# Seven half-size products for the second layer of a first mixture, with its weights narrowed in place

## The chip, the cores and the metric

The kernel runs on one core of one Trainium2 chip. The metric is the device time of one execution in microseconds (us); the number given for a kernel is the median of several executions.

## What is computed

Attention with a cluster mask, then a dense two-layer mixture (the "first mixture"), then a mixture of eight experts. Cut to what matters here:

```python
x = attention(q, k, v, centroids)            # (1536, 512)
h = x @ w_in                                  # w_in  (512, 2048)
g = h * (1.0 / (1.0 + np.exp(-h)))
x = g @ w_out                                 # w_out (2048, 512)
for e in range(8):                            # second mixture
    out += P[:, e:e+1] * (np.maximum(x @ w1[e], 0.0) @ w2[e])
```

All products are made in fp32 precision by splitting each factor into a part that TensorE's fp32r format holds and a rest: hi·hi + hi·lo + lo·hi, three matmuls for each product.

## The kernel before, in words

**Stages.** After the attention (L157 to L634) comes the first mixture, cut into NS1 = 4 blocks of 512 of the 2048 hidden features. A block is a loop over `u` (L1296): steps 0 to 6 are the first layer, steps 7 to 18 the second. Then follows the second mixture (L1353 on).

**First layer of a block.** The product of 512x512 weights with 512x1536 tokens is made by Strassen's scheme in Winograd's form: seven products of half size (256x256 by 256x768) in place of eight. `aproduct` (L679) issues one, 24 matmuls (L674); `AORD` (L131) is their order. `mfactor` (L145) makes a product's weight factor: `hi` by a ScalarE copy, `lo` by a VectorE subtraction. `sums1`, `sum4` and `sum3` (L135 to L143) make the weight sums on VectorE. `aevac` (L688) takes a product's three PSUM banks into the hidden blocks `hblk`, by ScalarE copies or VectorE additions. Products share PSUM sets of three banks: 1, 6, 7 and 4 one, 5 and 3 another, 2 a third.

**Second layer of a block.** Twelve output tiles (`ytile`, L724) of 512 columns by 128 features over all of the block's 512 hidden features, 12 or 16 matmuls each (L728), the ordinary product. `gsilu`, `ghi` and `glo` (L702 to L716) apply SiLU and split the hidden blocks. `total` (L743) adds a tile into the accumulator `acc1`: by ScalarE copies in block 0, by VectorE additions after that.

**Weights.** Each quarter of a weight block (128x512 values, `w_raw`, L81) is loaded by SyncE into one of three buffers and "narrowed" (`w_steps`, L89): the 64-bit numbers that the input holds become fp32 by bit operations. Steps `w0` (ScalarE, absolute value), `w1` (GpSimd, max and min), `w2` and `w3` (VectorE, shift and merge), `wb` and `wp0` (GpSimd, the low bits and their addition); for the second layer's weights then `wh` and `wp2`, the split.

**Order.** The instruction order on TensorE, VectorE, ScalarE and GpSimd is written out by hand: `put(s, u, f, ...)` (L755) hangs a step on slot `u` of block `s`, and the loop at L1295 issues slot after slot; each engine works through its own queue in that order and waits on semaphores. In the loop before, slots issue `mfactor`, `aevac` and `total` by rules (L1312 to L1321), then the hung steps, then the slot's product or tile.

Of the kernel before, what the change touches and what calls it, by code (L numbers as in the profile page):

```python
# [18 lines left out]
P = 128  # L19
# [20 lines left out]
def attention_moe_kernel(ctx, tc, kq, vp, cent, w_in, w_out, w_gate, w1, w2, out):  # L40
# [31 lines left out]
    raws, utp = {}, [wip]  # L72
# [16 lines left out]
    def w_steps(n, k, a=None):  # L89
# [16 lines left out]
        if not early:
            ts = nc.gpsimd.tensor_scalar

        def tail():
            if early:  # L110
                nc.scalar.activation(low, low, AF.Copy, scale=2.0**-29)
            else:
                ts(out=low, in0=low, scalar1=2.0**-29, scalar2=1.0, op0=ALU.mult, op1=ALU.mult)

        return dict(
            wb=tail,
# [5 lines left out]
            wp1=lambda: None,  # L122
            wh=lambda hi, lo: nc.scalar.copy(hi, a),
            wp2=lambda hi, lo: nc.vector.tensor_tensor(out=lo, in0=a, in1=r(hi), op=ALU.subtract),
# [6 lines left out]
    AORD = (1, 5, 6, 3, 7, 2, 4)  # L131
    AWHERE = {1: a11, 5: a21, 6: wsum, 3: a21, 7: a11, 2: a12, 4: a22}
# [6 lines left out]
    def sum4():  # L139
        nc.vector.tensor_tensor(out=a21, in0=a12, in1=wsum, op=ALU.subtract)  # L140
# [503 lines left out]
    utp.append(pool(rctx, "ut2", bufs=1, side="right"))  # L644
# [4 lines left out]
    wo_h, wo_l = (wop.tile([P, 4, 512], F32R, name=f"wo{c}") for c in "hl")  # L649
# [28 lines left out]

    def aproduct(s, i):  # L679
        p = AORD[i]  # L680
        if p in (1, 5, 2):
            asets[s, p] = [mps.tile([P, 512], F32, name=f"l{s}_{p}_{u}", tag="s") for u in range(3)]
        ps = asets[s, {6: 1, 7: 1, 4: 1, 3: 5}.get(p, p)]
        multiply(ps, groups1(i, wfac.pop((s, i)), yf[p]), p in (1, 5, 2))
# [32 lines left out]

    CHUNKS = (0, 2, 1)
# [5 lines left out]
    def ytile(s, t):  # L724
# [5 lines left out]
        if c < 2:  # L730
            for k in range(4):
                go(ps, wo_h, k, gh[:, c, k, :512], k == 0)
                go(ps, wo_l, k, gh[:, c, k, :512])
                go(ps, wo_h, k, gl[k // 2, c][:, k % 2, :512], False, k == 3)
# [470 lines left out]
    def narrow(n, k, keys):  # L1205
        if (n, k) not in quarters:
            quarters[n, k] = steps.pop(k + 4, None) if n == 1 else None
            quarters[n, k] = quarters[n, k] or w_steps(n, k, None if n % 2 else win[:, :, k * P : (k + 1) * P])
        for key in keys.split():
            quarters[n, k][key](*((wo_h[:, k : k + 1], wo_l[:, k : k + 1]) if key in ("wh", "wp2") else ()))  # L1210
            m = 4 * n + k + 3
            if key == ("wp1", "wp2")[n % 2] and 6 < m < 8 * NS1:
                w_raw(m // 4, m % 4)

    for s in range(NS1):
        n = 2 * s + 1
        if s == 0:
            put(s, 0, mfactor, 0, 1)
            put(s, 0, narrow, n, 0, "wh")
            put(s, 0, narrow, n, 1, "wh")  # L1220
            put(s, 0, narrow, n, 0, "wp2")
            put(s, 0, sum4)
            put(s, 0, narrow, n, 1, "wp2")
            put(s, 0, narrow, n, 2, "wb w0 w1")
            put(s, 1, narrow, n, 2, "w2 w3 wp0")
            put(s, 1, sum3)
            put(s, 1, split, 7, xb)
            put(s, 2, narrow, n, 2, "wh wp1 wp2")
            put(s, 2, narrow, n, 3, "wb w0 w1")
            put(s, 3, narrow, n, 3, "w2 w3 wp0")  # L1230
            put(s, 3, split, 4, xd)
            put(s, 4, narrow, n, 3, "wh wp1 wp2")
        else:
            put(s, 0, narrow, n, 0, "wh wp1")
            put(s, 0, sum4)
            put(s, 0, narrow, n, 1, "w2 w3 wp0")
            put(s, 0, narrow, n, 0, "wp2")
            put(s, 1, sum3)
            put(s, 1, narrow, n, 1, "wh wp1 wp2")
            put(s, 1, narrow, n, 2, "wb w0 w1")  # L1240
            put(s, 2, narrow, n, 2, "w2 w3 wp0")
            put(s, 2, narrow, n, 3, "wb w0 w1")
            put(s, 3, narrow, n, 2, "wh wp1 wp2")
            put(s, 3, narrow, n, 3, "w2 w3 wp0")
            put(s, 4, narrow, n, 3, "wh wp1 wp2")
        put(s, 4, gsilu, 3)
        put(s, 4, ghi, 3)
        put(s, 5, glo, s, 3)
        put(s, 5, gsilu, 7)
        put(s, 5, ghi, 7)  # L1250
        put(s, 6, glo, s, 7)
        put(s, 6, gsilu, 2)
        put(s, 6, ghi, 2)
        put(s, 7, glo, s, 2)
        put(s, 8, ghi, 4)
        put(s, 8, glo, s, 4)
        if s < NS1 - 1:
            n += 1
            for k in range(4):
                u = 8 + 2 * k  # L1260
                put(s, u, narrow, n, k, "wb w0 w1")
                put(s, u + 1, narrow, n, k, "w2 w3 wp0")
                put(s, u + 2, narrow, n, k, "wp1")
            n += 1
            put(s, 14, narrow, n, 0, "wb w0")
            put(s, 15, narrow, n, 0, "w1")
            put(s, 15, mfactor, s + 1, 0)
            put(s, 16, sums1)
            put(s, 17, mfactor, s + 1, 1)
            put(s, 17, narrow, n, 0, "w2 w3 wp0")  # L1270
            put(s, 17, narrow, n, 1, "wb w0")
            put(s, 18, narrow, n, 1, "w1")
# [21 lines left out]
    with tc.manual_schedule(engines={ENG.PE, ENG.DVE, ENG.Activation, ENG.Pool}):  # L1294
        for s in range(NS1):  # L1295
            for u in range(19):  # L1296
                if (s, u) == (0, 7):
                    acc1 = accp.tile([P, KC, NTOK], F32, name="acc1", tag="acc")
                if (s, u) == (NS1 - 1, 7):
# [12 lines left out]
                if 1 <= u <= 4:  # L1312
                    mfactor(s, u + 1)
                if 1 <= u <= 7:
                    aevac(s, u - 1)
                    if u == 5:
                        mfactor(s, u + 1)
                elif u > 7:
                    total(s, u - 8)
                elif s:  # L1320
                    total(s - 1, 11)  # L1321
# [287 lines left out]
```

## Time and profile before

| | us |
|---|---|
| median of 3 runs | 1433.44 (1433.26 to 1433.53) |
| the profiled execution | 1433.5 |
| its span, first to last instruction | 1431.7 |
| TensorE busy in the span | 1417.9 (99%) |

The profile is one execution. Each engine is a row of instructions with start and length; lengths of neighbours on one engine overlap, so what an instruction costs its queue is the distance from its start to the next start where the next one didn't wait. "Releaser" is the engine and line whose end let a waiting instruction start.

### The profile page before, as it was taken

Reading aid. Unit: us, or ns where it says so; the run is one execution under the profiler, and the core shown is the slowest. Engines: PE = TensorE matmul, PEld = TensorE weight load, DVE = VectorE, ACT = ScalarE, POOL = GpSimd, SP = SyncE. Lnnn points to the kernel's source line nnn. Section 1 sums busy time; section 2 is a strip of 40 time slices with the busy share of each in tenths; the row PEclk is TensorE's granted clock in tenths of the full one; section 3 lists DMA queues with packets and bytes.
Section 4 is the critical chain, followed back from the end, with each engine's and each line's share of the span. In section 5 each row is a group of like instructions: output and inputs, shape, how many; then the busy total and the mean of one; then the engine's idle time right before and its main releaser. Section 6 shows DMA issues by size and latency. Waiting matters only on the chain.

```text
span 1431.7 us, 25259 instructions
## 1 busy us (share of the span) xinstructions
PE 1417.9 (99%) x9685; PEld 1286.9 (90%) x9685; DVE 1141.1 (80%) x1887; ACT 973.1 (68%) x1876; POOL 441.4 (31%) x417
## 2 busy tenths in 40 slices
PE   8999999999999999999999999999999999999998
PEld 5777778888888899999999999999999999999998
DVE  7778888566756999997878878778788787887878
ACT  7777777653625476757768587686776867867764
POOL 6677754355361001302232222120211211202112
PEclk9999999999999999999999999999999999999999
DMA  7665621121121037758698897786956958669577
GB/s 209 184 182 146 195 66 45 48 86 60 59 95 38 2 102 142 121 115 184 107 194 134 157 177 132 139 140 116 172 97 119 162 96 169 113 120 163 92 149 133
DMA packets 136313, 177.49 MB, mean 124 GB/s; under 512 B 6272, under 2 KB 108672, under 8 KB 136192
## 3 DMA queue, kind: packets, MB, share of 16 engines
q0 software_dynamic: 83856, 87.56, 40.5%
q1 hardware_dynamic: 51648, 87.85, 19.9%
q8 instruction: 76, 1.25, 0.4%
q10 hardware_dynamic: 688, 0.46, 0.1%
q14 instruction: 45, 0.37, 0.1%
HBM read 65.36 MB, written 88.87 MB: 108 GB/s over the span
## 4 chain that ended last, share of the span: by engine, by line
PE 93%; DVE 3%; ACT 1%; issue 1%; POOL 1%; DMA 0%; DVEq 0%; POOLq 0%; ACTq 0%
PE b L674 27%; PE a L674 23%; PE y L728 9%; PE l L674 8%; PE b L1060 4%; PE q L1040 4%; PE t L349 4%; PE av L372 4%; PE r L1040 4%; PE s L305 2%; PE s L307 2%; DVE m L314 1%; POOL p L340 1%; DVE acc L1141 1%; DVE al L772 0%
## 5 line engine op out<-in xcount | busy, mean ns | idle before, releaser
L674 PE MATMUL b<-wfh,ah 128*128 128x256 f32 x1164 | 330.7, 284 | 0.1
L674 PE MATMUL b<-wfh,al 128*128 128x256 f32 x1164 | 329.2, 283 | 0.0
L674 PE MATMUL b<-wfl,ah 128*128 128x256 f32 x1164 | 329.2, 283 | 0.0
L1167 POOL DMA_DIRECT2D out_dram<-acc x87 | 126.5, 1779 | 535.2 <-ACT acc L1158 509.9
L1158 ACT ACTIVATE acc<-b,Pg 128x256 f32<-128x256 f32 x564 | 222.2, 538 | 6.2 <-PE b L1060 5.2
L674 PEld LDWEIGHTS b<-wfh,ah 128*128 128x128 f32 x1164 | 222.9, 192 | 0.5 <-ACT acc L1158 0.3
L674 PEld LDWEIGHTS b<-wfl,ah 128*128 128x128 f32 x1164 | 223.1, 192 | 0.0
L674 PEld LDWEIGHTS b<-wfh,al 128*128 128x128 f32 x1164 | 223.1, 192 | 0.0
L674 PE MATMUL a<-xfl,wfh 128*128 128x512 f32 (+1 forms) x640 | 215.8, 337 | 0.0
L674 PE MATMUL a<-xfh,wfl 128*128 128x512 f32 (+1 forms) x640 | 215.5, 337 | 0.0
L674 PE MATMUL a<-xfh,wfh 128*128 128x512 f32 (+1 forms) x640 | 215.4, 337 | 0.0
L1093 ACT CAST ah<-h 128x768 fp32r<-128x768 f32 x160 | 134.7, 854 | 111.1 <-DVE h L1189 53.3
L1080 ACT COPY h<-a 128x512 f32<-128x512 f32 x192 | 113.6, 618 | 102.4 <-PE a L674 96.7
L772 DVE TENSOR_TENSOR al<-h,ah 128x768 fp32r<-128x768 f32 x160 | 151.4, 954 | 28.8 <-ACT ah L1093 23.7
L674 PEld LDWEIGHTS a<-xfh,wfl 128*128 128x128 f32 x640 | 121.0, 189 | 13.0
L674 PEld LDWEIGHTS a<-xfh,wfh 128*128 128x128 f32 x640 | 121.1, 189 | 11.5 <-issue 0.6
L674 PEld LDWEIGHTS a<-xfl,wfh 128*128 128x128 f32 x640 | 121.0, 189 | 10.4
L323 ACT ACTIVATE p<-s,m 128x768 f32<-128x768 f32 x96 | 86.5, 903 | 35.2 <-DVE m L314 30.8
L340 POOL TENSOR_SCALAR p<-p,rec 128x768 f32<-128x768 f32 x95 | 85.8, 915 | 51.5 <-DVE rec L328 40.9
L314 DVE TENSOR_REDUCE m<-s 128x1 f32<-128x768 f32 x96 | 90.0, 951 | 13.9 <-PE s L307 13.5
L769 DVE TENSOR_TENSOR h<-q,h 128x384 f32<-128x384 f32 x112 | 61.0, 555 | 35.4 <-PE q L1040 33.1
L772 DVE TENSOR_TENSOR wfl<-w0r,wfh 128x512 fp32r<-128x512 f32 x96 | 64.6, 688 | 28.7 <-ACT wfh L885 28.7
(256 smaller groups left out, 3370.0 us busy)
## 6 DMA issues: line engine op xcount, KB each, us to landing
out_dram<-acc POOLq DMA_DIRECT2D x91, 768.0 KB, 9.1
w0r<-in_w_dram SPq DMA_DIRECT2D x16, 1024.0 KB, 5.6
w1r<-in_w_dram SPq DMA_DIRECT2D x16, 1024.0 KB, 8.6
qk<-qk SPq DMA_DIRECT2D x45, 192.0 KB, 3.5
wr<-in_w_in_dram SPq DMA_DIRECT2D x16, 512.0 KB, 3.8
wr<-in_w_out_dram SPq DMA_DIRECT2D x16, 512.0 KB, 3.5
first_out<-acc POOLq DMA_DIRECT2D x10, 768.0 KB, 8.6
raw<-in_kq_dram SPq DMA_DIRECT2D x16, 384.0 KB, 4.4
```

Of the source, the lines that this page charges most:

```text
L314: nc.vector.tensor_reduce(out=m, in_=tiles[i]["s"][:, :S], axis=AX.X, op=ALU.max, negate=True)
L323: nc.scalar.activation(t["p"], t.pop("s")[:, :S], AF.Exp, bias=t.pop("m"), accum_out=chunks[c]["sum"][:, j, 0:1])
L340: e.tensor_scalar(out=p, in0=p, scalar1=chunks[c]["rec"][:, j : j + 1], scalar2=1.0, op0=ALU.mult, op1=ALU.mult)
L674: nc.tensor.matmul(ps[u][:, cols], lhsT=lf(i, k), rhs=rt(j, k), start=fresh and u not in opened, stop=k == 1 and q == 2, skip_group_check= ...
L728: nc.tensor.matmul(out, lhsT=w[:, k, d * P : (d + 1) * P], rhs=g, start=first, stop=last, skip_group_check=True)
L769: e.tensor_tensor(out=out, in0=in0, in1=in1, op=op)
L772: e.tensor_tensor(out=lo, in0=x, in1=r(hi), op=ALU.subtract)
L1040: nc.tensor.matmul(ps, lhsT=quad_lhs(s, q, a, four), rhs=(x4 if four else xq)[b][:, XQ[q]], start=j == 0 and q in (1, 2, 5), stop=j == 2, ...
L1080: act.copy(bank(t, u), ps[u])
L1093: act.copy(hi, x)
L1158: act.mul(t[:, 2 * u + m], z[:, m], Pg[:, 6 * i + 2 * u + m, e : e + 1])
L1167: gps.dma_start(out=to, in_=t, accum_op=ALU.add)
```

## The change

In blocks 0, 1 and 2 the second layer is also made of seven half-size products (`bproduct`), in the loop's steps 7 to 13; the block is 14 steps long. Block 3 keeps the twelve tiles, with another order of the inner index.

- **Operands.** The product's token side is the hidden block after SiLU or a difference of such blocks (`hsum`, VectorE, in place), split by `hhi` (ScalarE) and `hlo` (VectorE) into two operand buffers used in turn (halves of `gh`). The weight side is a quarter of `win2`, where the narrowed weights now stand whole, or a sum (`bsums1`, `bsum4`, `bsum3`, VectorE), split by `mhi` and `mlo`, seven times a block.
- **Results.** `bevac` copies a product's three banks in four pieces on ScalarE: in block 0's products 1, 5, 6 and 4 straight into `acc1`, else into a ring of five buffers (`outs`), from which two accumulating DMAs (GpSimd's queue, 128 rows of 768 fp32 each) add them into `acc1`. VectorE's additions of `total` fall away in blocks 1 and 2.
- **Narrowing** (from the seventh quarter on): the ScalarE step scales in place, GpSimd clamps in place, and VectorE merges with two `scalar_tensor_tensor` (shift-or, and-or). GpSimd's addition `wp0` and the buffer `ut` fall away for these quarters; one quarter of each block is scaled on GpSimd (`wg`).
- **Orders.** `AORD` becomes (1, 2, 6, 5, 7, 3, 4), and the sum `sum4` lands in another block accordingly. In block 0 the first two quarters are copied to `win2` (`bring`).

```diff
@@ w_steps
+        if 4 * n + k > 5:
+            ts, v, top = nc.gpsimd.tensor_scalar, high.bitcast(F32), 122879.9921875 * 2.0**-112
+            stt = nc.vector.scalar_tensor_tensor
+            return dict(
+                wb=lambda: ts(out=low, in0=low, scalar1=2.0**-29, scalar2=7.0, op0=ALU.mult, op1=ALU.min),
+                w0=lambda: nc.scalar.activation(v, v, AF.Copy, scale=2.0**-112),
+                wg=lambda: ts(out=v, in0=v, scalar1=2.0**-112, scalar2=1.0, op0=ALU.mult, op1=ALU.mult),
+                w1=lambda: ts(out=v, in0=v, scalar1=-top, scalar2=top, op0=ALU.max, op1=ALU.min),
+                w2=lambda: stt(out=low, in0=high, scalar=3, in1=low, op0=ALU.logical_shift_left, op1=ALU.bitwise_or),
+                w3=lambda: stt(out=ai, in0=high, scalar=0x80000000, in1=low, op0=ALU.bitwise_and, op1=ALU.bitwise_or),
+                wh=lambda hi, lo: nc.scalar.copy(hi, a),
+                wp2=lambda hi, lo: nc.vector.tensor_tensor(out=lo, in0=a, in1=r(hi), op=ALU.subtract),
+            )
...
-    AORD = (1, 5, 6, 3, 7, 2, 4)
+    AORD = (1, 2, 6, 5, 7, 3, 4)
...
+    BORD = (1, 5, 6, 3, 7, 2, 4)
+    BWHERE = {1: b11, 5: b21, 6: wsum2, 3: b21, 7: b11, 2: b12, 4: b22}
+    BTO = {1: (0, 1), 5: (1, 0), 6: (0, 0), 3: (0, 0), 7: (1, 0), 2: (0, 1), 4: (1, 1)}
+    BX = {1: (0, 1), 5: (0, 1), 6: (0, 1), 3: (1, 0), 7: (0, 0), 2: (1, 1), 4: (1, 1)}
...
+    def hhi(j, m):
+        nc.scalar.copy(operand(j)[0][:, m], hblk[BX[BORD[j]]][:, m])
+
+    def hlo(j, m):
+        hi, lo = operand(j)
+        nc.vector.tensor_tensor(out=lo[:, m], in0=hblk[BX[BORD[j]]][:, m], in1=r(hi)[:, m], op=ALU.subtract)
...
+        multiply(bsets[s, SHARE.get(p, p)], groups1(1, wfac.pop((s, 7 + j)), operand(j)), p in OPEN, True)
+
+    PIECES = ((1, 0, 256, 0, 512), (1, 256, 512, 1, 0), (0, 0, 512, 0, 0), (2, 0, 512, 1, 256))
...
+        for u, a, b, m, c in pieces:
+            z = (to if straight else moved[s, j])
+            z = z[:, m, c : c + b - a] if straight else z[m][:, c : c + b - a]
+            nc.scalar.copy(z, ps[u][:, a:b])
+            if not straight and u in (0, 2):
+                nc.gpsimd.dma_start(out=to[:, m], in_=moved[s, j][m], accum_op=ALU.add)
...
+        go(8, hsum, X, Z, X, 0)
+        go(8, hsum, X, Z, X, 1)
+        go(8, mhi, s, 9)
+        go(8, mlo, s, 9)
+        go(8, bevac, s, 0, PIECES[:2])
+        for m in range(2):
+            go(8, hhi, 2, m)
+            go(8, hlo, 2, m)
+        go(8, narrow, n + 1, 2, "wg w1 wb")
+        go(8, bevac, s, 0, PIECES[2:])
...
+        go(12, narrow, n + 1, 0, "w2 w3")
+        for m in range(2):
+            go(12, hhi, 6, m)
+            go(12, hlo, 6, m)
+        go(12, mhi, s, 13)
+        go(12, mlo, s, 13)
+        go(12, bevac, s, 4)
+        go(13, narrow, n + 1, 1, "w2 w3")
+        go(13, narrow, n + 1, 2, "w2 w3")
+        go(13, mhi, s + 1, 0)
+        go(13, mlo, s + 1, 0)
+        go(13, narrow, n + 1, 3, "w0")
+        go(13, bevac, s, 5)
+        go(13, narrow, n + 1, 3, "wb w1")
+        go(13, aopen, s + 1, 1)
...
+            for u in range(19 if s == NS1 - 1 else 14):
...
                 if u < 7:
                     aproduct(s, u)
+                elif direct:
+                    ytile(s, u - 7)
                 else:
-                    ytile(s, u - 7)
+                    bproduct(s, u - 7)
```

At the head of a following block (slot 0) stand `bevac` of the seventh product, the next factor, `w2 w3` of quarter 3, `sums1` and the next quarter's `w0 w1 wb`. A raw load is issued by SyncE after the `w3` of the quarter three before it.

## Rows read from the trace of the kernel before

**Rows 1.** The page: span, and busy time of each engine with its share.
```profile
span 1431.7 us, 25259 instructions
PE 1417.9 (99%) x9685; PEld 1286.9 (90%) x9685; DVE 1141.1 (80%) x1887; ACT 973.1 (68%) x1876; POOL 441.4 (31%) x417
```

**Rows 2.** The chain that ended last, block 0's second and block 1's first layer: start, length, what.
```profile
263.70 32.99 PE y L728 x160
296.69 29.22 PE l L674 x168
```

**Rows 3.** Busy time by stage, block 1's two layers: stretch, engines, granted clock, DMA.
```profile
296.60:325.70 29.10, 29.10 (x169) 25.71 (x168) 19.48 (x29) 19.27 (x32) 12.10 (x10) 1.00 0.24 73
325.70:358.90 33.20, 33.20 (x163) 28.05 (x162) 20.02 (x30) 9.74 (x16) 21.16 (x16) 1.00 0.20 64
```

**Rows 4.** ScalarE in order of time, block 2: start, length, line, operation.
```profile
363.06 0.62 ACT L148 CAST vh<-wsum 128x512 fp32r<-128x512 f32 x1 [4.83 <-PE l L674]
363.58 1.55 ACT L696 COPY h<-l 128x512 f32<-128x512 f32 x3
365.01 0.67 ACT L123 CAST woh<-wr 128x512 fp32r<-128x512 f32 x1
365.57 0.68 ACT L117 ACTIVATE u<-wr 128x512 f32<-128x512 f32 x1
...
380.27 1.56 ACT L710 CAST gh<-h 128x768 fp32r<-128x768 f32 x2
381.73 0.62 ACT L148 CAST vh<-win 128x512 fp32r<-128x512 f32 x1
```

**Rows 5.** ScalarE's 256-column copy from PSUM: duration in ns, least, median, most.
```profile
L396 ACT CAST yh<-av x18: 358/372/373, 83.3 to 234.3; 128x256 fp32r<-128x256 f32 x18
```

**Rows 6.** VectorE in order of time, block 2.
```profile
360.80 0.69 DVE L120 SCALAR_TENSOR_TENSOR wr<-wr,u 128x512 uint32<-128x512 uint32 x1
361.41 0.69 DVE L124 TENSOR_TENSOR wol<-wr,woh 128x512 fp32r<-128x512 f32 x1
...
382.37 0.69 DVE L149 TENSOR_TENSOR vl<-win,vh 128x512 fp32r<-128x512 f32 x1 [0.63 <-ACT vh L148]
382.98 1.82 DVE L716 TENSOR_TENSOR gl<-h,gh 128x768 fp32r<-128x768 f32 x2
384.72 1.88 DVE L700 TENSOR_TENSOR h<-l,h 128x512 f32<-128x512 f32 x3
386.51 3.75 DVE L716 TENSOR_TENSOR gl<-h,gh 128x768 fp32r<-128x768 f32 x4
```

**Rows 7.** VectorE beside GpSimd at two places, in order of time.
```profile
241.09 1.41 POOL L121 TENSOR_TENSOR wr<-wr 128x512 uint32<-128x512 uint32 x1 [2.63 <-DVE wr L120]
241.53 3.12 DVE L420 TENSOR_TENSOR yf<-xs,yf 128x768 fp32r<-128x768 f32 x2
242.60 1.24 POOL L113 TENSOR_SCALAR wr<-wr 128x512 uint32<-128x512 uint32 x1
...
371.56 1.92 POOL L118 TENSOR_SCALAR u<-u 128x512 f32<-128x512 f32 x1
372.05 0.69 DVE L149 TENSOR_TENSOR vl<-win,vh 128x512 fp32r<-128x512 f32 x1 [2.50 <-ACT vh L148]
```

**Rows 8.** GpSimd's narrowing steps and its casting DMA's issue: durations, least, median, most.
```profile
L118 POOL TENSOR_SCALAR u<-u x26: 1915/1917/2422, 236.5 to 433.8; 128x512 f32<-128x512 f32 x26
L113 POOL TENSOR_SCALAR wr<-wr x26: 640/662/1243, 204.5 to 433.0; 128x512 uint32<-128x512 uint32 x26
L185 POOL DMA_DIRECT2D qk<-raw x14: 557/588/798, 14.3 to 176.3; - x14
```

**Rows 9.** Issue to landing: raw weight loads (L86), then the casting SBUF-to-SBUF DMA (L185).
```profile
DMA to landing us min/median/max: 3.3/3.7/6.2
DMA to landing us min/median/max: 3.1/4.8/5.9
```

**Rows 10.** The queue of GpSimd's DMAs: packets, MB, share of 16 engines' span.
```profile
q0 software_dynamic: 83856, 87.56, 40.5%
```

More of the change, by code (lines that the diff above doesn't have):

```diff
@@ L677, in attention_moe_kernel, with aopen @@
     asets = {}
+    OPEN = (1, 5, 2)
+    SHARE = {6: 1, 7: 1, 4: 1, 3: 5}
+    def aopen(s, p):
+        asets[s, p] = [mps.tile([P, 512], F32, name=f"l{s}_{p}_{u}", tag="s") for u in range(3)]
     def aproduct(s, i):
         p = AORD[i]
[L681 to L684, printed above, removed]
+        if p in OPEN and (s, p) not in asets:
+            aopen(s, p)
+        multiply(asets[s, SHARE.get(p, p)], groups1(i, wfac.pop((s, i)), yf[p]), p in OPEN)
     CB = {1: (0, 1), 5: (1, 0), 6: (0, 0), 3: (0, 0), 7: (1, 0), 2: (0, 1), 4: (1, 1)}
@@ new lines, in operand, with bopen, bproduct @@
+    def operand(j):
+        return [ghs[:, 4 * (j % 2) + 2 * q : 4 * (j % 2) + 2 * q + 2] for q in range(2)]
+    def hhi(j, m):
[3 more added lines that the diff above has]
+        nc.vector.tensor_tensor(out=lo[:, m], in0=hblk[BX[BORD[j]]][:, m], in1=r(hi)[:, m], op=ALU.subtract)
+    def bopen(s, p):
+        bsets[s, p] = [mps.tile([P, 512], F32, name=f"y{s}_{p}_{u}", tag="s") for u in range(3)]
+    def bproduct(s, j):
+        p = BORD[j]
+        if p in OPEN and (s, p) not in bsets:
+            bopen(s, p)
+        multiply(bsets[s, SHARE.get(p, p)], groups1(1, wfac.pop((s, 7 + j)), operand(j)), p in OPEN, True)
@@ new lines, in attention_moe_kernel, with bevac @@
+    PIECES = ((1, 0, 256, 0, 512), (1, 256, 512, 1, 0), (0, 0, 512, 0, 0), (2, 0, 512, 1, 256))
+    moved = {}
+    def bevac(s, j, pieces=PIECES):
+        p = BORD[j]
+        ps = bsets[s, SHARE.get(p, p)]
+        d, h = BTO[p]
+        to = acc1[:, 2 * d : 2 * d + 2, h * S : (h + 1) * S]
+        straight = s == 0 and p in (1, 5, 6, 4)
+        if not straight and (s, j) not in moved:
+            moved[s, j] = [outs[(outn[0] + m) % 5] for m in range(2)]
+            outn[0] += 2
+        for u, a, b, m, c in pieces:
[4 more added lines that the diff above has]
+                nc.gpsimd.dma_start(out=to[:, m], in_=moved[s, j][m], accum_op=ALU.add)
@@ L730, in ytile @@
         if c < 2:
[L731 to L732 removed]
+            for k in (2, 3, 0, 1):
+                go(ps, wo_h, k, gh[:, c, k, :512], k == 2)
                 go(ps, wo_l, k, gh[:, c, k, :512])
[L734 removed]
+            for k in (2, 3, 0, 1):
+                go(ps, wo_h, k, gl[k // 2, c][:, k % 2, :512], False, k == 1)
         else:
@@ L1211, in narrow @@
             m = 4 * n + k + 3
-            if key == ("wp1", "wp2")[n % 2] and 6 < m < 8 * NS1:
+            if key == ("wp2" if n == LASTN else "w3") and 6 < m < 8 * NS1:
                 w_raw(m // 4, m % 4)
-    for s in range(NS1):
[L1216 to L1232, printed above, removed]
-        else:
[L1234 to L1272, printed above, removed]
@@ L1295, in attention_moe_kernel @@
         for s in range(NS1):
-            for u in range(19):
+            for u in range(19 if s == NS1 - 1 else 14):
                 if (s, u) == (0, 7):
                     acc1 = accp.tile([P, KC, NTOK], F32, name="acc1", tag="acc")
+                    stay = glp.tile([P, 2, S], F32, name="stay", tag="h")
+                    outs += [stay[:, 0], stay[:, 1]]
                 if (s, u) == (NS1 - 1, 7):
@@ L1311, in attention_moe_kernel @@
                     w_load(7)
[L1312 to L1318, printed above, removed]
+                direct = s == NS1 - 1
+                if direct and u == 2:
+                    wo_h, wo_l = (wop.tile([P, 4, 512], F32R, name=f"wo{c}", tag=f"wo{c}") for c in "hl")
+                if direct and u > 7:
                     total(s, u - 8)
-                elif s:
-                    total(s - 1, 11)
                 for f, args in slots.pop(19 * s + u, ()):
```

188 lines of the change are left out of this document (160 added, 28 removed).

## The prediction

> **What bounds the kernel now.** The page comes first: TensorE is busy for 99% of the span, VectorE for 80%, ScalarE for 68% [rows 1]. A busy TensorE proves little by itself, so the chain of waits comes next: in the first mixture it stays on TensorE without a break, 32.99 us for a second layer (`ytile`, L728) and 29.22 us for a first layer (L674) [rows 2], and this pair repeats in every block. The table by stage says the same and adds what stood beside: in a first layer VectorE was busy 19.5 of 29.1 us and ScalarE 19.3, in a second layer 20.0 and 9.7 of 33.2; the granted clock is 1.00 of full speed, 2.4 GHz [rows 3]. So this stage ends when TensorE's matmuls end, and the other engines have room: 39.5 of 62.2 us on VectorE, 29.0 on ScalarE.
>
> **The saving on TensorE.** The first layer is already seven half-size products, so one costs 29.22 / 7 = 4.17 us [rows 2]. A second layer has as many multiplications; as seven products with the same tile shapes it takes another 29.22 us. That is 32.99 - 29.22 = 3.77 us a block, 11.3 us in three blocks. The new products go through the contraction by halves (first all of its first 128 features, then the rest); the matmuls are the same 24, and I add nothing. If nothing waits, the profiled 1433.5 us, which is the median's 1433.44 within 0.1, becomes 1422.1. This is the floor; everything below takes from it.
>
> **What the products ask of ScalarE.** Costs are start-to-start distances. A 512-wide split costs 363.58 - 363.06 = 0.52 us, a 512-wide copy from PSUM 1.43 / 3 = 0.48, a narrowing step 365.57 - 365.01 = 0.56, a 768-wide split (381.73 - 380.27) / 2 = 0.73 [rows 4]. A 256-wide copy lasts 0.37 [rows 5]; less the 0.10 by which neighbours overlap [rows 4], 0.27. A block of 14 units of 4.17 us, 58.4 us, holds 14 `mhi` (7.3), 14 `hhi` (10.2), 7 `bevac` of two 256-wide and two 512-wide copies (10.5), 12 first-layer copies (5.8), 6 SiLUs at the price of a 768-wide split (4.4) and 7 narrowing steps (3.9): 42.1 us, 72%. Units 8 to 12 are the fullest: 1.50 + 1.46 + 0.52 = 3.5 of 4.17 us. ScalarE fits.
>
> **What they ask of VectorE.** A 512-wide operation costs 382.98 - 382.37 = 0.61 us, the bit operation too (361.41 - 360.80), a 768-wide one 1.74 / 2 = 0.87, an addition from PSUM 1.79 / 3 = 0.60 [rows 6]. A block holds 9 additions (5.4), 14 `mlo` (8.5), 8 weight sums (4.9), 14 `hlo` (12.2), 8 `hsum` (7.0) and 16 merges, two for each quarter (9.8): 47.8 us, 82%. That is above what this engine carried here before, though 12 additions of `total` leave it. By unit it is 4.15, 3.6, 4.1, 3.8, 3.8, 4.1 in units 6 to 11, 23.6 us in 25.0: no unit above 4.17, and almost no room. Units 1 and 4 need about half, and there a lag is made up.
>
> **VectorE beside GpSimd.** Two 768-wide subtractions took 3.12 us where 1.82 is usual [rows 6, 7]: the first began in a GpSimd addition (`wp0`, until 242.50), the second met the step behind it. Of the 1.30 us lost, 0.97 lie in front of 242.50 and 0.33 belong to the second step. The clamp `w1` is kinder: a subtraction inside its 1.92 us took its usual 0.69 [rows 7]. The addition falls away; clamp and scaling stay, 17 a block with `wg`. The lower bound is 0 each, the upper the whole instruction, 1.92 and 0.66 [rows 8]. I take 0.33, from the row that shows the same step: 5.6 us, and VectorE stands at 53.4 of 58.4 us. Three quarters fall in units 5 to 8, so some 2 us come on top of units that have only 1.4 spare. Walking the queues by hand, a unit's operands are ready 0.7 to 3 us ahead of the product, and a stall gives the lag back. I charge 0.5 us a block, 1.5 in all.
>
> The Trainium skill's page "SBUF — State Buffer", section "SBUF: two separate sides", speaks against this change: VectorE instructions with two SBUF inputs and GpSimd instructions that read SBUF lock one pair of ports against each other for the whole instruction. By that rule the clamp would also stop VectorE for its whole length, which the second place of rows 7 does not show; the first place agrees. What it would make of the sum is the first slower rival below.
>
> **The seam between blocks.** Three loads run ahead. Quarter 3 of the next first layer is loaded only after `w3` of quarter 0, at the start of unit 12, and its sums are needed at unit 16, the next block's third product. The chain in between: load 3.7 us [rows 9], scaling 0.56, the sixth product's `bevac` ahead in ScalarE's queue 1.5, the DMA issues ahead in GpSimd's 0.59, then 0.66 and 1.92 [rows 8], two merges 1.22, `sums1` 1.22, split 0.52 and 0.61: 12.5 us. From the end of that `w3`, about 1.2 us into unit 12, there are 15.5, some 14 with VectorE's lag. The new waits: ScalarE waits for the load at `w0`, with `bevac` queued behind it and TensorE's next product waiting for those banks; GpSimd's `wb` and `w1` queue behind DMA issues; VectorE's merges wait for `w1`, with `sums1` behind. Worst case: the load takes 6.2 us [rows 9] and the scaling, now a minimum instead of a multiplication, costs as much as the clamp (1.92 for 0.66 [rows 8]): 3.8 us more, 2.3 past the 14. Strided in-place clamps have no row; between 0.66 and 1.92 I take 1.92. I charge 0.5 us at each of three seams, 1.5 in all.
>
> **The accumulating DMAs.** 14 a block in blocks 1 and 2, 6 in block 0, of 393 KB. No row shows one within SBUF. Nearest is the casting DMA, 384 KB within SBUF on the same queue: 0.59 us to issue [rows 8], 4.8 to land [rows 9]. The ring gives a buffer back after two products at the earliest, some 8 us; so at 4.8 they cost ScalarE nothing. The other end is the queue's own average: 87.56 MB in 40.5% of 1431.7 us, 151 GB/s, 2.6 us each [rows 1, 10]. I take the first, and nothing for them: that queue mostly adds into DRAM.
>
> **At no cost.** Block 0's beginning: product 2 moves to second place and needs the last attention output, whose split stands in front of it in the queues already; its own first factor needs no sum. Block 3 keeps 32.99 us. Its tiles start with the inner index whose operands come first, hidden by its 11 us of matmuls for four tiles; uncovered, the last split would cost one 768-wide pass, 0.9. Second mixture: unchanged.
>
> **Sum.** 1433.4 - 11.3 + 1.5 + 1.5 = 1425.1 us.
>
> **The rivals.**
> (A) The seam is late: 2.3 us at each of three seams and 0.5 a block, 8.4 us of stalls, so 1430.5. For it: the long chain over five queues, 6.2 us seen for a load. Against it: the median load, 3.7.
> (B) The lock holds for all of each GpSimd instruction; slower. GpSimd would run 8 x 2.58 + 0.66 + 14 x 0.59 = 29.6 us a block [rows 8], and VectorE has two SBUF inputs in 42.4 of 58.4 us: 73%, 21.6 us lost, 69.4 us a block against 62.2. Twice 7.2, with block 0 even: 1448. It decides from 62.2 - 47.8 = 14.4 us lost in a block. Rows 7's second place speaks against it.
> (C) The DMAs are slow; slower. 14 x 2.6 = 36.4 us must pass in the 29.2 from one unit 8 to the next block's first unit; 7.2 us twice on top of my sum gives 1439.5. It decides where a DMA takes over 2.1 us; the ring then holds `bevac`, and TensorE its banks.
> (D) It doesn't do what it says: products by halves cost as much as the tiles they replace (4.71 us each): 1433.
>
> **How the numbers follow.** Forecast 0.63, (A) 0.17, (B) 0.06, (C) 0.09, (D) 0.05. Likeliest: 1425.1. The range, 1421.8 to 1431.0, goes from no stall at all to past (A); (B), (C) and (D), 0.20, lie outside. Faster or slower is meant by over 0.2% (2.9 us), about what a measurement tells from no change. The forecast and two thirds of (A) are faster, 0.74; (D) and the rest of (A) 0.11; (B) and (C) 0.15.
>
> **What the profile will show.** Right: the chain has stretches of about 58.4 us a block up to block 3, TensorE's idle time there is 1 us a block, VectorE's busy share is the highest of this stage. Wrong in the VectorE step: 768-wide subtractions far over 0.95 us beside clamps. Wrong at the seam: TensorE waits in front of a block's first or third product for ScalarE or VectorE. Wrong on DMAs: ScalarE waits for a DMA in `bevac`, or landings over 8 us. Block 3's or the second mixture's length changing would make the sum wrong altogether.

## The result and the profile after

| | median | runs, or range | against before |
|---|---|---|---|
| before | 1433.35 us | 1433.24 to 1433.53 | |
| changed | 1453.18 us | 1451.86 to 1456.93 | 1.0142, 95% interval 1.0123 to 1.0162 |
| forecast | 1425.1 us | 1421.8 to 1431.0 | |

The change makes the kernel 19.8 us slower, 28.1 us from the forecast and well outside its range; a slower kernel had been given 0.15. The profiled execution took 1451.86 us; its span is 1450.1 us. The page answers to [rows 1]: TensorE is busy a little less, every other engine more.

```profile
span 1450.1 us, 25558 instructions
...
PE 1414.8 (98%) x9709; PEld 1279.2 (88%) x9709; DVE 1186.0 (82%) x1926; ACT 1018.1 (70%) x1974; POOL 486.6 (34%) x428
```

Shares over the whole span hide the place, so the second view is the table by stage, cut at the layers of the first mixture, for comparison with [rows 3]. Columns: stretch, length, then busy time (and instructions) of TensorE, its weight loads, VectorE, ScalarE and GpSimd, granted clock, DMA share, GB/s. The rows are block 0's first and second layer, then blocks 1 and 2 likewise, block 3's first layer, and the head of its tiles. Line numbers are from here on those of the changed kernel.

```profile
234.00:262.40 28.40, 28.40 (x165) 25.14 (x164) 21.15 (x32) 21.53 (x35) 12.04 (x6) 1.00 0.24 74
262.40:294.50 32.10, 30.51 (x172) 25.86 (x170) 29.73 (x36) 23.89 (x46) 15.79 (x10) 1.00 0.30 59
294.50:326.70 32.20, 29.85 (x168) 25.72 (x169) 24.70 (x34) 20.81 (x37) 26.60 (x14) 1.00 0.52 147
326.70:359.70 33.00, 30.69 (x170) 25.73 (x169) 29.48 (x36) 23.39 (x46) 20.74 (x16) 1.00 0.60 113
359.70:392.90 33.20, 30.84 (x167) 25.59 (x168) 23.02 (x33) 20.05 (x36) 26.82 (x16) 1.00 0.70 181
392.90:426.70 33.80, 30.74 (x171) 25.79 (x169) 30.35 (x37) 24.10 (x47) 21.63 (x16) 1.00 0.58 110
426.70:466.60 39.90, 32.05 (x169) 25.68 (x169) 21.50 (x32) 20.45 (x37) 24.35 (x14) 1.00 0.61 165
466.60:470.20 3.60, 2.13 (x6) 0.92 (x6) 3.34 (x5) 3.60 (x6) 0.00 (x0) 1.00 0.00 0
```

The clock is 1.00 (2.4 GHz) in all of them, so the time is waits. A second layer takes 32.1 to 33.8 us where 29.2 was forecast and 33.0 stood before: the saving is eaten in the very layer that should bring it. First layers, which the change hardly touches on TensorE, grow from 29.2 to 32 and 33 us, and block 3's to 39.9. This stage's last layer, the tiles, runs without a break from 470.2 us on, six matmuls after its start, where before it began at 450.3; from there to the end of the span both take about 980 us.

Whom TensorE waits for says little by itself: the list of waits puts 10.1 us down to ScalarE's split of a weight factor, `vh` (`mhi`, L150). What ScalarE waited for ahead of that split has to be followed in its own queue, and then in GpSimd's. GpSimd from 234 to 476 us, by line and operation (busy us, mean ns | idle before):

```profile
L110 POOL TENSOR_SCALAR wr<-wr 128x512 f32<-128x512 f32 x26 | 58.0, 2232 | 42.7 <-ACT wr L108 41.8
L107 POOL TENSOR_SCALAR wr<-wr 128x512 uint32<-128x512 uint32 x26 | 56.9, 2188 | 2.0
...
L791 POOL DMA_DIRECT2D acc<-rest x14 | 13.9, 1080 | 24.1 <-ACT rest L789 20.0 <-DMA acc<-stay 4.1
```

and the DMAs issued from 234 to 430 us (KB each, median us from issue to landing; `rest`, `stay` and `outx` are the ring's buffers), below the share of their queue in these 196 us:

```profile
q0 software_dynamic: 4216, 11.53, 32.9%
...
wr<-in_w_out_dram SPq DMA_DIRECT2D x11, 512.0 KB, 7.7
acc<-rest POOLq DMA_DIRECT2D x14, 384.0 KB, 6.8
acc<-stay POOLq DMA_DIRECT2D x12, 384.0 KB, 8.4
acc<-outx POOLq DMA_DIRECT2D x6, 384.0 KB, 6.4
```

Three things stand there. The scaling of the low bits (L107, `wb`), 0.66 us before [rows 8], takes 2.19 us with its minimum. An accumulating DMA's issue lasts 1.08 us (0.6 from start to start where the next follows at once) and it lands after 6.4 to 8.4 us, medians by buffer. And GpSimd spent 20.0 us in front of the issues in the third row, 33.6 with those of the other buffers, waiting for ScalarE's copies, with narrowing steps queued behind. One case of each kind, in order of time (start, length, what, and in brackets the wait before it and for whom):

```profile
334.41 2.31 POOL L110 TENSOR_SCALAR wr<-wr 128x512 f32<-128x512 f32 x1
336.80 2.13 POOL L107 TENSOR_SCALAR wr<-wr 128x512 uint32<-128x512 uint32 x1
339.00 0.91 POOL L791 DMA_DIRECT2D acc<-rest  x1
...
343.18 0.37 ACT L789 COPY rest<-y 128x256 f32<-128x256 f32 x1 [2.56 <-DMA acc<-rest]
...
344.92 0.62 ACT L150 CAST vh<-win 128x512 fp32r<-128x512 f32 x1
...
345.59 0.51 PE L685 MATMUL y<-gh,vh 128*128 128x256 f32 x2 [0.73 <-ACT vh L150]
...
352.11 0.86 POOL L791 DMA_DIRECT2D acc<-outx  x1 [4.03 <-DMA acc<-rest]
```

The first DMA of block 1's second layer is issued at 339.00, behind 4.4 us of narrowing; the copy that filled its buffer had ended at 335.2. The buffer is wanted again at 340.6; ScalarE waits 2.56 us for it, the split behind that copy is late, and TensorE waits. This is the prediction's sign "ScalarE waits for a DMA in `bevac`". The other, "landings over 8 us", stands a little further on, but not on this DMA: of the four issued one behind the other from 339.00 on, the first lands after 4.1 us and the last, issued at 340.69, after 8.6:

```profile
L791 POOL DMA_DIRECT2D acc<-rest x1: 911/911/911, 339.0 to 339.0; - x1
DMA to landing us min/median/max: 4.1/4.1/4.1
...
L791 POOL DMA_DIRECT2D acc<-stay x1: 1914/1914/1914, 340.7 to 340.7; - x1
DMA to landing us min/median/max: 8.6/8.6/8.6
```

Later GpSimd itself waits 4.03 us: product 3's DMA adds to where product 6's has not landed.

Block 3 has a circle of its own:

```profile
443.16 0.69 DVE L112 SCALAR_TENSOR_TENSOR wr<-wr 128x512 uint32<-128x512 uint32 x1
...
443.89 0.65 ACT L113 CAST woh<-wr 128x512 fp32r<-128x512 f32 x1 [5.05 <-DVE wr L112]
...
447.89 0.64 ACT L150 CAST vh<-win 128x512 fp32r<-128x512 f32 x1
448.56 0.69 DVE L154 TENSOR_TENSOR vl<-win,vh 128x512 fp32r<-128x512 f32 x1 [4.70 <-ACT vh L150]
448.58 0.73 PE L685 MATMUL l<-yf,vh 128*128 128x512 f32 x2 [1.86 <-ACT vh L150]
```

ScalarE stood 5.05 us in front of `wh` (L113) for VectorE's merge; behind it came the next product's `vh`; and VectorE then stood 4.70 us for that `vh`, with the next merge queued behind. Two engines take turns where they should run side by side.

### The profile page after: what moved, and what is told of

It reads as the page before. It is cut to its first block, busy times and chain, and to the rows that moved or that the text cites. A ratio compares the mean times of both kernels' runs of the same rounds, so it can differ in the third digit from the quotient of the medians.

```text
span 1450.1 us, 25558 instructions
## 1 busy us (share of the span) xinstructions
PE 1414.8 (98%) x9709; PEld 1279.2 (88%) x9709; DVE 1186.0 (82%) x1926; ACT 1018.1 (70%) x1974; POOL 486.6 (34%) x428
## 4 chain that ended last, share of the span: by engine, by line
PE 65%; DVE 1%; ACT 1%; issue 0%; DVEq 0%; ACTq 0%
PE b L685 27%; PE a L685 23%; PE b L1136 4%; PE q L1116 4%; PE r L1116 4%; PE y L803 2%; DVE acc L1217 1%; PE a L1130 0%; DVE al L848 0%; PE gl L1048 0%; ACT gh L726 0%; DVE h L845 0%; ACT acc L1234 0%; DVE h L1271 0%; DVE wfl L848 0%
```

## The experiments

Theory 1: block 3's order, with `wh` in the same slot as its merges, costs most of the loss. Theory 2: GpSimd's queue does, (2a) by the minimum in `wb`, (2b) by the accumulating DMAs that land late in a ring of five staging buffers. Edits are to the changed kernel (1453.2 us). The times of all are in the table at the end of this section.

### One cause at a time

`e1_split_later`:

```diff
-        done = ("w2 w3 wh", "wp2") if last else ("w2 w3", "")
+        done = ("w2 w3", "wh wp2") if last else ("w2 w3", "")
```

(and the call for quarter 2 goes from slot 4 to slot 5).

> The changed kernel (1453.2 us), with one thing moved: in block 3 the split of a narrowed quarter (wh, wp2) is hung one slot behind its merges (w2, w3), not in the same slot. Theory 1 (in block 3 ScalarE and VectorE wait for each other in a circle: wh waits for w3, w3 stands behind mlo, mlo waits for mhi, and mhi stands behind wh): block 3's first layer shrinks from 39.8 us to some 30, and the time to 1440 to 1444. Theory 2 (GpSimd's queue and the accumulating DMAs are late, in every block): the wait returns at another place, and the time stays above 1450.

Measured: 1448.84 us, 4.3 less. Block 3's first layer shrinks from 39.8 to 33.9 us, not to 29.2, and the rest stays: neither theory alone.

`e2_cheap_scale`, two multiplications in place of a multiplication and a minimum; the factor is a little smaller, so that the largest value needs no cap:

```diff
-  wb=lambda: ts(out=low, in0=low, scalar1=2.0**-29, scalar2=7.0, op0=ALU.mult, op1=ALU.min),
+  wb=lambda: ts(out=low, in0=low, scalar1=7.49 * 2.0**-32, scalar2=1.0, op0=ALU.mult, op1=ALU.mult),
```

> The changed kernel with GpSimd's scaling of the low bits as two multiplications (the factor a little smaller, so that it rounds to at most 7), not a multiplication and a minimum. Theory 2a (the minimum makes this step 2.2 us where it was 0.66, and GpSimd's queue carries the DMA issues late): the step falls to 0.7 us, and with 1.4 us less for each of 8 quarters the time falls by 6 to 10 us, to 1443 to 1447. Theory 2b (the DMAs' own length in the ring is what counts): 0 to 3 us, 1450 to 1453. Theory 1 alone: 0 to 2 us.

Measured: 1445.29 us, 7.9 less. The step itself, from 234 to 476 us, against 2188 ns above:

```profile
L107 POOL TENSOR_SCALAR wr<-wr 128x512 uint32<-128x512 uint32 x26 | 22.7, 872 | 2.0
```

`e3_no_adds` leaves the accumulating DMAs out, so part of the sum is missing:

```diff
-            if not straight and u in (0, 2):
-                nc.gpsimd.dma_start(out=to[:, m], in_=moved[s, j][m], accum_op=ALU.add)
```

> The changed kernel with the accumulating DMAs into acc1 left out (the ring is still filled by ScalarE; the first mixture's sums are therefore incomplete). Theory 2b (the ring gives its buffers back late): ScalarE's 10.0 us of waits for DMAs in bevac vanish, and the time falls by 8 to 12 us, to 1441 to 1445. Theory 2a: GpSimd's narrowing is as late as before, so 3 to 5 us, about 1449. Theory 1: block 3's 14 us stay in both.

Measured: 1434.29 us, 18.9 less and more than expected, with the minimum still in place. So the minimum costs nearly only because DMA issues stand in the same queue: 2a and 2b are one cause.

`e4_three_edits` joins the first two and moves slot 8's narrowing behind the second half of `bevac`:

```diff
-        go(8, narrow, n + 1, 2, "wg w1 wb")
         go(8, bevac, s, 0, PIECES[2:])
+        go(8, narrow, n + 1, 2, "wg w1 wb")
```

> Three edits together: the split of block 3 one slot later, the scaling as two multiplications, and slot 8's narrowing on GpSimd hung behind the second half of bevac, so that the DMA issues stand ahead of it. If theories 1 and 2a are both right and add up, 1428 to 1436; if one wait only takes another's place, above 1440.

Measured: 1452.44 us, nothing won. The narrowing now stands in front of the second product's DMAs, which go out at 347.61 where the first ones went at 335.15:

```profile
336.31 1.81 DVE L763 TENSOR_TENSOR gh<-h,gh 128x768 fp32r<-128x768 f32 x2
336.34 7.58 POOL L109 TENSOR_SCALAR wr<-wr 128x512 f32<-128x512 f32 x1
...
343.64 1.09 DVE L763 TENSOR_TENSOR gh<-h,gh 128x768 fp32r<-128x768 f32 x1 [0.24 <-ACT gh L759]
...
347.61 1.81 POOL L791 DMA_DIRECT2D acc<-stay  x2
```

ScalarE then waited 5.63 us for a buffer. But the order alone does not explain this. The scaling `wg` in the second row takes 7.58 us here and 5.25 in block 2, against 1.24 in block 0: 6.3 and 4.0 us too much, about what the second layers of these two blocks lose against `e5` below (37.3 for 31.1 us and 36.1 for 31.9). Both long scalings begin 0.03 us behind an operation of VectorE and end 0.5 us after VectorE's first gap since then (343.41 and 412.91): GpSimd looks shut out for as long as VectorE works without a gap. No run takes this apart, and elsewhere GpSimd's steps ran in between VectorE's, so the cause stays open, and with it how much of the loss the order itself made.

### Two causes, and what of a DMA costs

`e5_split_and_scale` is the first two edits without the third.

> The changed kernel with the first two edits together (block 3's splits into high parts one slot later; low bits scaled by two multiplications instead of a multiplication and a minimum), and slot 8 as it was, so that against the run of three edits only the moved narrowing is missing. If the two causes are separate, their gains add: 1453.2 - 4.3 - 7.9 = 1441.0 us, 1439 to 1443 us. If it was the combination that the ring of staging buffers took back, the time stays over 1447 us, and the moved narrowing had no part in the loss of the third edit.

Measured: 1442.14 us. The two gains add (4.3 + 7.9 = 12.2 expected, 11.0 seen); the third edit cost 10.3, the two long scalings included.

`e6_split_no_adds` has the later split and no accumulating DMAs.

> The changed kernel without the accumulating DMAs (that part of the sum is left out) and with block 3's splits one slot later: both things gone that held TensorE. If the saving of 3.77 us a block is real and was only covered by the ring and by block 3's circle, the time falls under the kernel before, to 1427 to 1430 us (1434.3 of the run without the adds, less the 5 to 6 us that its block 3 spends over 29.2 us). If products by halves give nothing on TensorE, or something else takes the place, it stays at 1433 us or above.

Measured: 1427.73 us, ratio 0.9958 (0.9943 to 0.9973). This is the forecast's floor with nothing late on GpSimd. The rows are blocks 1 and 2, layer by layer, and block 3's first layer (columns as above; the 0.3 us from 355.2 to 355.5 belong to block 1's second layer):

```profile
295.80:325.10 29.30, 29.30 (x169) 25.87 (x168) 24.22 (x34) 20.24 (x35) 24.89 (x11) 1.00 0.34 108
325.10:355.20 30.10, 29.84 (x169) 25.68 (x168) 29.39 (x36) 24.05 (x47) 13.22 (x6) 1.00 0.11 35
355.50:384.80 29.30, 29.30 (x170) 25.88 (x169) 24.26 (x34) 20.56 (x35) 25.27 (x13) 1.00 0.33 107
384.80:415.10 30.30, 30.06 (x171) 25.81 (x170) 29.18 (x36) 24.40 (x49) 14.19 (x7) 1.00 0.11 35
415.10:444.40 29.30, 29.30 (x169) 25.87 (x168) 22.16 (x33) 21.07 (x37) 20.18 (x9) 1.00 0.34 120
```

`e7_plain_moves` and `e8_plain_moves_from_sync` keep the DMAs' number and bytes, but copy instead of adding, so the sum is incomplete again; the second issues them on SyncE's queue:

```diff
-  nc.gpsimd.dma_start(out=to[:, m], in_=moved[s, j][m], accum_op=ALU.add)
+  nc.gpsimd.dma_start(out=to[:, m], in_=moved[s, j][m])      # e7
+  nc.sync.dma_start(out=to[:, m], in_=moved[s, j][m])        # e8
```

> The changed kernel with its accumulating DMAs made plain copies, from the same queue on GpSimd, in the same number and order (the addition is left out). If accumulating, which reads its destination too, is what makes a DMA take 6.4 to 8.4 us to land, the ring comes free in time and the run lands near the one without these DMAs, 1434 to 1440 us. If it is the queue and GpSimd's time to issue (some 1.1 us each, behind its own narrowing), it stays at 1448 to 1454 us.

> As the run with plain copies, but issued on SyncE's queue, which has only the weight loads (the addition is left out). GpSimd then has only its narrowing and no issue stands behind a narrowing step. If GpSimd as the issuer is the cause, 1434 to 1439 us, well under the plain copies from GpSimd's queue; if the data's way through the DMA engines is, about as the plain copies from GpSimd.

Measured: 1441.38 and 1434.94 us. Issue to landing in e7 (in e8 3.2 and 3.5):

```profile
acc<-rest POOLq DMA_DIRECT2D x14, 384.0 KB, 3.4
acc<-stay POOLq DMA_DIRECT2D x13, 384.0 KB, 4.0
```

That splits the DMAs' cost: adding instead of copying 1453.2 - 1441.4 = 11.8 us, GpSimd's queue instead of SyncE's 1441.4 - 1434.9 = 6.4, moving the bytes 1434.9 - 1434.3 = 0.6, which is within the spread of the two. Block 3's order is the rest, 1434.3 - 1427.7 = 6.6. That the four make up the 25.5 us between the changed kernel and `e6` is arithmetic; each price holds at its place in this order. Block 3's order was worth 4.3 in `e1`, with everything else still there, and the 7.9 of the minimum (`e2`) is no fifth part, for `e6` has the minimum still. The granted clock, told at `e14` below, blurs the smaller of these prices.

### Relief for GpSimd's queue

`e9_low_bits_first` puts `wb` ahead of the clamp `w1`, on top of `e5` (`"w0 wb w1"` for `"w0 w1 wb"`, everywhere).

> The run with later splits and cheap scaling, and in each narrowing the low bits' scaling on GpSimd put ahead of the clamp, which waits for ScalarE's scaling of the high bits (54.6 us of waits for it on GpSimd in that run from 234 to 476 us). If GpSimd's queue still holds TensorE after the first two edits, each narrowing ends up to 0.9 us earlier and the time falls from 1442.1 to 1438 to 1441 us. If what is left is only the landing of the accumulating DMAs, it stays within 1 us of 1442.1.

Measured: 1441.92 us, no change. From 234 to 476 us GpSimd waits 33.2 us in front of the clamp in place of 54.6, but now 12.5 for the raw loads of `w_out` in front of `wb`, and in front of its DMA issues as long as before (30.2 us for 30.9 in the row of `rest`).

`e10_product6_by_vector` and `e11_products_6_and_4_by_vector` go on from there and let VectorE add some products of blocks 1 and 2 to the accumulator out of PSUM, with no staging and no DMA:

```diff
+            if s and p in (6,):        # e11: (6, 4)
+                nc.vector.tensor_tensor(out=to[:, m, c : c + b - a], in0=ps[u][:, a:b], in1=to[:, m, c : c + b - a], op=ALU.add)
+                continue
```

> As the run with low bits first, and in blocks 1 and 2 the second layer's product 6 added to the accumulator by VectorE out of PSUM in place of ScalarE's copies and two accumulating DMAs (4 of 34 go). If the DMAs' landing and the wait of product 3's DMA for product 6's (same destination) hold GpSimd and the ring, the time falls by 2 to 5 us against that run. If VectorE, at some 85% of the time in these blocks, is the next bound, the time stays or rises by up to 3 us: the sums and low parts behind the adds come about 2 us later.

> As the run before with product 4's evacuation, the last of the block and at its seam, by VectorE as well (8 of 34 accumulating DMAs go). If the ring is the bound at the seam, another 2 to 4 us less; if VectorE is, whose merges, sums and subtractions stand at the seam, some 2 us more at each of two seams, 4 us in all.

Measured: 1443.48 us (its runs, 1442.1 to 1444.9, overlap those of `e9`: undecided, and not the 2 to 5 us less that were expected) and 1438.26 us. The two products together gave 3.7 us against `e9`, product 4 at the block's seam 5.2 against `e10`, and VectorE had room for their additions.

`e12_seam_order` moves one narrowing ahead of two DMA issues, `e13_seam_and_slot7` also reorders slot 7:

```diff
-        go(13, bevac, s, 5)
         go(13, narrow, n + 1, 3, "wb w1")
+        go(13, bevac, s, 5)
```

```diff
-        for m in range(2):
-            go(7, hhi, 1, m)
-            go(7, hlo, 1, m)
+        go(7, hhi, 1, 0)
+        go(7, hlo, 1, 0)
         go(7, mhi, s, 8)
         go(7, mlo, s, 8)
+        go(7, hhi, 1, 1)
+        go(7, hlo, 1, 1)
```

> The run with products 6 and 4 by VectorE, and in slot 13 the last narrowing's low-bit scaling and clamp put ahead of product 2's evacuation, so that on GpSimd they no longer stand behind two DMA issues that wait for ScalarE's copies (4.5 to 4.9 us). If GpSimd's order at the seam holds the third product of the next block (1.67, 1.37 and 0.54 us of waits for its high part, and 0.4 us behind each), these stalls go: 1438.3 - 4.5 = 1433.5 to 1435 us. If the landing of the DMAs does, they only start 2.9 us later and the time stays at 1438 us or rises.

> As the run before, and in slot 7 the second product's low weights subtracted between the two 768-wide operand subtractions instead of behind both. If VectorE's order holds product 2 of the second layer (1.66, 0.97 and 0.97 us of waits for its low part), another 2 to 3 us less: 1431 to 1433 us, under the kernel before. If it is VectorE's total work, beside GpSimd's clamps, the wait comes back one half product later and nothing is won.

Measured: 1432.98 and 1433.20 us. The seam's order gives 5.3 us. GpSimd at the seam of blocks 1 and 2, and the product that waits for it, in `e11`:

```profile
359.83 0.87 POOL L794 DMA_DIRECT2D acc<-stay  x1 [4.46 <-ACT stay L792]
360.37 1.23 POOL L794 DMA_DIRECT2D acc<-rest  x1
361.67 0.65 POOL L107 TENSOR_SCALAR wr<-wr 128x512 uint32<-128x512 uint32 x1
362.38 1.99 POOL L110 TENSOR_SCALAR wr<-wr 128x512 f32<-128x512 f32 x1
...
368.68 0.73 PE L685 MATMUL l<-yf,vh 128*128 128x512 f32 x2 [0.95 <-ACT vh L150]
```

and in `e12`, where the two steps use the time that was spent waiting:

```profile
355.98 0.65 POOL L107 TENSOR_SCALAR wr<-wr 128x512 uint32<-128x512 uint32 x1 [2.63 <-DMA wr<-in_w_in_dram]
356.71 1.99 POOL L110 TENSOR_SCALAR wr<-wr 128x512 f32<-128x512 f32 x1
358.64 0.92 POOL L794 DMA_DIRECT2D acc<-stay  x1
...
365.66 0.62 PE L685 MATMUL l<-yf,vh 128*128 128x512 f32 x2
```

Slot 7's order wins nothing. TensorE's waits for the low weights of the second product (1.46, 0.76 and 0.29 us in blocks 0 to 2 of `e12`) shrink to 0.15 in block 0 and vanish in blocks 1 and 2, and waits for the activations' low part in the third product come (0.63, 0.30 and 0.30).

`e14_block3_order` puts quarter 2's split ahead of the SiLU in block 3's slot 5; `e15_whole_products` then takes the halves out of the second layer's products.

```diff
-        go(5, gsilu, 7)
         if last:
             go(5, narrow, n, 2, done[1])
+        go(5, gsilu, 7)
```

```diff
-  multiply(..., groups1(1, wfac.pop((s, 7 + j)), operand(j)), p in OPEN, True)
+  multiply(..., groups1(1, wfac.pop((s, 7 + j)), operand(j)), p in OPEN)
```

> As the run with the seam's order, and in block 3's slot 5 the split of weight quarter 2 put ahead of the SiLU, which waits 2.9 us for VectorE's adds; VectorE's low part and the last quarter's merges stand behind that split (1.58 us of wait) and the first tile behind them (1.50 us for its low weights). If ScalarE's order holds the head of the tiles, it comes 1.5 to 2 us earlier: 1431 to 1431.7 us, under the kernel before (1433.6). If the wait for the high part of the activations (0.95 and 0.44 us) takes its place, 1432.5 to 1433 us.

> As the run before, with the second layer's products in the order of the first layer's, not by halves of their inner dimension. In the trace a product by halves takes 4.24 us and one of the first layer 4.08 or 4.26 us in turn, 4.17 on the mean: if only that counts, 21 x 0.07 = 1.5 us less. If the second half's operands come late, as VectorE's subtractions in the traces do (they end within 1 us of the product that needs them), each product waits about 0.9 us for them: up to 15 us more.

Measured: 1431.57 us (0.9987, 0.9978 to 0.9996) and 1431.78 us. The head of the tiles came earlier, as expected; `e14` and `e15` are the only complete versions under the kernel before, by 0.1%. Not all of that step is order, as the rows from 450 to 460 us show, first `e12`, then `e14`:

```profile
450.00:460.00 10.00, 9.99 (x37) 7.81 (x37) 7.64 (x10) 4.63 (x8) 0.00 (x0) 0.83 0.00 0
450.00:460.00 10.00, 9.81 (x42) 7.82 (x43) 7.05 (x9) 4.05 (x7) 0.00 (x0) 1.00 0.00 0
```

In the 10 us before, at the head of the tiles, TensorE was busy 8.30 us in `e12` and 9.80 in `e14`. Behind that `e12`'s granted clock fell for a while from 2.4 to 1.2 GHz. A mean of 0.83 makes about 3.4 us at the lower level and 1.7 us lost, an estimate from the row. Such dips, behind waits of TensorE, stand from 230 to 500 us in the profiles of ten runs (`e1` to `e4`, `e7` to `e10`, `e12`, `e13`) and in none of the changed kernel, `e5`, `e6`, `e11`, `e14` and `e15`. By the same estimate they cost 1.7 us in most, 3.4 in `e3` and `e7` and some 5 in `e1` and `e4`. Each is one execution, but a difference of a few us between runs of the two kinds is not the edit's alone.

Products without halves still take 4.24 us, so the 0.07 us over the first layer's mean are not the halves' price; nor did the operands come too late for them. The trace of `e15` shows what is left: a product of the second layer has its twelve 512-wide matmuls by themselves (2.80 us) and its twelve 256-wide ones (1.44), while the first layer turns the order round from product to product, so that 24 of one width stand together and take 5.47 and 2.88 us.

| kernel | us | ratio to before (95% interval) |
|---|---|---|
| e1 later split | 1448.84 | 1.010 to 1.013 |
| e2 cheap scaling | 1445.29 | 1.0073 to 1.0103 |
| e3 no adding DMAs | 1434.29 | 0.9999 to 1.0019 |
| e4 both and slot 8 | 1452.44 | 1.0117 to 1.0147 |
| e5 both | 1442.14 | 1.0046 to 1.0076 |
| e6 later split, no adding DMAs | 1427.73 | 0.9943 to 0.9973 |
| e7 plain copies, GpSimd | 1441.38 | 1.0039 to 1.0069 |
| e8 plain copies, SyncE | 1434.94 | 1.0002 to 1.0021 |
| e9 e5 and low bits first | 1441.92 | 1.0040 to 1.0074 |
| e10 and product 6 by VectorE | 1443.48 | 1.0053 to 1.0083 |
| e11 and product 4 by VectorE | 1438.26 | 1.0021 to 1.0043 |
| e12 and the seam's order | 1432.98 | 0.9985 to 1.0004 |
| e13 and slot 7 | 1433.20 | 0.9987 to 1.0006 |
| e14 e12 and block 3's order | 1431.57 | 0.9978 to 0.9996 |
| e15 and whole products | 1431.78 | 0.9980 to 0.9998 |

## Why the prediction was wrong

**The saving on TensorE** was right. With neither late DMAs nor block 3's circle (`e6`) a second layer of blocks 1 and 2 takes 30.4 us against 32.99 [rows 2]; 29.2 and 0.5 of waits were forecast. Rival (D) falls: a product took 4.24 us, not 4.71. The floor came out at 1427.7 for 1422.1. In the profile of `e6` (1428.65 us) the three second layers take 31.3, 30.5 and 30.4 us from first matmul to first matmul, 4.5 more than three times 29.22: 21 x 0.07 = 1.5 us for the products, where "I add nothing" stood, and waits and small gaps, 1.6 in block 0 and 0.8 and 0.7 in blocks 1 and 2. The part from the tiles on is 0.8 us longer, and the attention ended 1.2 us later than in the profile before.

**ScalarE and VectorE** were right. In block 2 of `e6` ScalarE is busy (20.56 + 24.40) / 59.6 = 75% (72% forecast), and VectorE in block 1 24.22 + 29.39 = 53.6 us, 53.4 forecast. The lock beside GpSimd has the size that was taken from [rows 7], of which rival (B) made more:

```profile
328.14 2.55 POOL L110 TENSOR_SCALAR wr<-wr 128x512 f32<-128x512 f32 x1
...
328.75 2.27 DVE L763 TENSOR_TENSOR gh<-h,gh 128x768 fp32r<-128x768 f32 x2
...
330.77 2.11 POOL L107 TENSOR_SCALAR wr<-wr 128x512 uint32<-128x512 uint32 x1
```

In the changed kernel two subtractions began inside one clamp and ended in the next step: 2.27 us for 1.82 [rows 6], 0.45 lost over the two steps, where 0.33 a step was taken. By the Trainium skill's page "SBUF — State Buffer", section "SBUF: two separate sides", the first would have stood until 330.69, where the clamp ends; it and the second were over at 331.02, so the trace does not show that rule in full. The two long scalings of `e4` are the one place in these runs where GpSimd seems to have stood through several of VectorE's operations.

**The accumulating DMAs** are the step that failed first: "so at 4.8 they cost ScalarE nothing", and "nothing for them" in the sum. In its place `e3` showed 18.9 us. The price for one DMA was not the mistake: the first of a bunch lands after 4.0 to 4.1 us (issued at 284.00, 339.00 and 406.07). Those right behind it wait their turn: the four of 339.00 to 340.69 land 4.1, 5.7, 7.1 and 8.6 us after their issues, 2.1 us one after the other. Four plain copies in `e7` (336.59 to 338.3) land after 2.6, 3.3, 3.7 and 4.2 us, 1.1 apart. What makes an addition slower was not tested. And the 8 us until a buffer is wanted were not there: `rest` was full at 335.2 and wanted at 340.6. Had its DMA gone out at once, it would have landed at 339.3, in time (an estimate from its 4.1 us); GpSimd's narrowing held the issue back until 339.00. So late issues made ScalarE wait, and bunched the DMAs that then landed late.

By the Trainium skill's page "DMA: Bandwidth & Descriptors", section "Anatomy of one DMA — SWDGE (gpsimd) path", 2.0 us and 0.9 for 393 KB make an estimate of 2.9. The plain copies come near it (2.6 us for the first of a bunch); the adding ones, at 4.0 and more, do not.

Rival (C) named the place and the sign. Its condition was over 2.1 us of queue time a DMA, and 32.9% of 196 us over 32 DMAs are 2.0: spread evenly, as (C) counted them, they would have fitted. They came in bunches, and there the ring held `bevac` all the same.

**GpSimd had no budget.** ScalarE and VectorE were added up unit by unit; GpSimd, 31% busy on the page [rows 1], was not. Its only sum, 29.6 us a block, stands in rival (B) and serves the lock there; in block 1 of the changed kernel it was busy 26.60 + 20.74 = 47.3 us. The seam's sum held the DMA issues ahead of `wb` and `w1` as "0.59", as if they were ready. They wait for ScalarE's copies, in order: 4.46 us of waiting and two issues in the fence of `e11`, and `e12` wins 5.3 us by that order alone. The chain was otherwise well measured: in `e6` no first layer waits at its seam.

**The minimum in `wb`** was known with both ends (0.66 and 1.92) but charged at the seam alone, at the quick end. It takes 2.19 us, 8 times a block, ahead of DMA issues: 7.9 us of time (`e2`). Where no DMA stands behind it, little can be its own: `e6` has it still, and there TensorE waits 1.5 us in the whole stage.

**"Block 3 keeps 32.99 us"** failed too, ahead of the tiles that it speaks of: block 3's first layer took 39.9 us in place of 29.2. The sum looked at the tiles' inner order and not at what moved in ScalarE's queue: `wh` now waits for two merges on VectorE, with the next `vh` behind. That cost 4.3 us with the other causes there, 6.6 without.

## What to carry to other kernels

Add up every engine that the change gives work to, waits included, however idle the page shows it: an engine at a third of its time can hold the kernel if a step that waits stands in front of a step that others wait for. An unseen kind of DMA must be priced in the bunches in which it will be issued, not alone and not by its queue's average, and set against the time from when its issue can really go out until its buffer is wanted. Before trying a cure by reordering, ask what the moved step will now stand in front of, and look in the trace whether anything else moved: narrowing put ahead of two DMA issues won 5.3 us at the seam, and narrowing put behind two lost 10.3 in slot 8, with two steps in it that took four and six times their usual length.

## What the runs showed of the hardware

A `tensor_scalar` on GpSimd with a minimum as its second operation takes 2.2 us on 128x512, with two multiplications 0.87 in the same place. A DMA within SBUF that adds kept GpSimd busy for about 1.0 us and a plain one for 0.55 (mean of 34), but from one issue to the next both take 0.5 to 0.6. Alone, the adding one lands after 4.0 us and the plain one after 2.6; in a bunch the adding ones land 2.1 us apart and the plain ones 1.1. The raw loads of `w_out`, on another queue, landed after 7.7 us beside the adding DMAs, 3.5 without (`e3`), and 4.0 (`e7`) and 4.6 (`e8`) beside plain copies of the same bytes. After a wait of TensorE its granted clock could fall for a while from 2.4 to 1.2 GHz (`e12`, 0.83 over 10 us), so a wait can cost more than its length.
